# Two-bank score conversions, merged shifts and a spread-out second normalisation in a fused attention and routed-MLP kernel

## The chip, the cores and the metric

The kernel runs on one NeuronCore of a Trainium2 chip. Its time is the device time of one execution in microseconds (us), given as the median over several runs. The profile is of one execution of its own, whose time stands beside the others; "span" is the time from its first to its last instruction. Engine names are those of the profile: PE is TensorE, ACT is ScalarE, DVE is VectorE, POOL is GpSimd, SP is SyncE, which here only issues DMAs.

## The reference

One sequence of 2048 rows of width 448 (bf16) passes through two blocks.

```python
x = A_x
h  = x + A(layernorm(x))         # A: 16 heads of width 28 that share one k and one v
h2 = h + B(layernorm(h))         # B: a routed MLP for 8 rows of the 2048

# A
q = (x @ wq) in 16 heads; k = x @ wk; v = x @ wv          # k, v: 2048 x 28
o = softmax(q k^T / sqrt(28)) v, per head; return concat(o) @ wo
# B
r = x @ w_r; idx = the 8 rows with the largest r
y = (silu(x[idx] @ w_gate) * (x[idx] @ w_up)) @ w_down * sigmoid(r[idx])
return x + scatter_add(zeros, idx, y)                     # x is the normalised h here
```

So every output row is h + layernorm(h), and 8 rows get an MLP result on top.

## The kernel before, in words

**The order of the work.** `_main` only describes operations: engine, code, a duration, the keys it reads and writes, a priority (the planned time of the event that made it). `_Graph.plan` then runs a list scheduler over these durations and so fixes one static order for each engine; `finish` and `emit` place the semaphore waits. An instruction whose wait lasts longer than planned holds everything that stands behind it on its engine. DMAs are issued by SP in such an order too, and the two gathers and the last scatter by POOL.

**The blocks.** The attention is cut into 16 blocks `b`: a quarter of the queries (`b // 4`, 512 of them) by a group of 4 heads (`b % 4`). A block has 16 tiles `j` of 128 keys; planned time counts 16 units to a block. For each tile PE makes the scores of 4 heads in two halves `p` (two matmuls each, into a pair of PSUM banks), one engine turns scores into bf16 probabilities, and PE multiplies them by V, accumulating in the bank `acc_bank(b)`. A row of ones in V gives the sum of the probabilities, `l`. There are two ways to make the probabilities:

- ACT tiles (`act_unit`, line 845): two exponentials of 128x1024 each, one for each half, over banks 0 and 1 or 2 and 3 in turn; four matmuls with V.
- DVE tiles (`dve_unit`, `shift`, lines 858 and 864): K carries a scale that makes the clamped, converted int16 the bit pattern of a bf16 near the exponential. Each half lies in banks 4 and 5 and takes two conversions of 128x512. Three shifts then add 32, 64 and 96 to the 128x2048 integers of level 0 and write levels 1 to 3, and all four levels are multiplied by four differently scaled copies of V, 16 matmuls in all. The buffer `Y` has three places.

`groups[b]` says how many of a block's 16 tiles are DVE tiles: 4, but 3 in blocks 5, 9 and 13.

**After a block** (`post_block`): DVE copies the accumulator to `Ot` (line 636), a DMA writes its four rows `l` to DRAM, another reads them back as 128x16 (`Lc`), DVE folds them into a running minimum and maximum `Lmn`, `Lmx` (lines 640, 642; they decide at the end whether an exact version of everything has to run) and takes reciprocals, two more DMAs spread these over the partitions (`Rb`), and POOL multiplies (line 648, `On`).

**After four blocks** (`out_proj`, four row tiles `t` of 128 rows): PE multiplies by wo, DVE adds x (`hbuf`), takes mean and variance, POOL raises to the power -0.5 (line 670), DVE makes the output row `outf`, a normalised row `xn` in bf16 (line 680), and the router value `r` of each row. The four tiles of blocks 0 to 3, of 4 to 7 and of 8 to 11 stand about 2 units apart in blocks 5, 9 and 13. After the fourth, one DMA writes `outf` to the output and one writes `xn` to a DRAM scratch.

**The router.** After 12 row tiles (`first_row`, `first_max`), PE brings 1536 router values to 12 partitions, three DMAs lay them out as one row of 1536, and DVE's MAX8 and FIND_INDEX8 (lines 713, 715) find the best 8. In block 15 (`second_top`) the 8 indices go to 8 partitions (`idc`, line 727) and POOL gathers (line 735) these rows from the output (`extc`) and from the scratch (`xnc`). The last 512 rows are handled in the tail: normalised there, searched together with the best 8, then the MLP for 8 rows and a scatter by POOL.

`last_w` (lines 741, 749) computes w_r times wo and w_r times x for the tail.

Of the kernel before, what the change touches and what calls it, by code (L numbers as in the profile page):

```python
# [7 lines left out]
ALU = mybir.AluOpType  # L8
# [222 lines left out]
def _main(nc, G, sb, ps, psb, flag, scr, xs, A_x, A_wq, A_wk, A_wv, A_wo, B_w_r, B_w_gate, B_w_up, B_w_down, out,  # L231
# [79 lines left out]
    r12 = sb("r12", [12, 128], F32)  # L311
    r_row = xnF[0:1, 0:3072].bitcast(F32)
# [11 lines left out]
    iota_n = sb("iota_n", [128, 5], F32)  # L324
    iota_i = sb("iota_i", [128, 2, NT], I32)
# [95 lines left out]
    for i in range(4):  # L421
# [26 lines left out]
    G.op(DV, lambda e: e.memset(Lmn[:, :], 1.0), 90, writes=["Lmn"])  # L448
    G.op(DV, lambda e: e.memset(Lmx[:, :], 1.0), 90, writes=["Lmx"])
# [158 lines left out]
    def post_block(b):  # L608
        g, qb, rb = b % 4, b // 4, b % 2
        u = 16 * (b + 1) + 2.6  # L610
# [24 lines left out]
        else:  # L635
# [4 lines left out]
        G.op(DV, lambda e: e.tensor_tensor(Lmn[:, :], Lmn[:, :], Lc[:, rb, :], ALU.min), 85,  # L640
             reads=["Lmn", ("Lc", rb)], writes=["Lmn"])
        G.op(DV, lambda e: e.tensor_tensor(Lmx[:, :], Lmx[:, :], Lc[:, rb, :], ALU.max), 85,
             reads=["Lmx", ("Lc", rb)], writes=["Lmx"])
        if not last:
            G.op(DV, lambda e: e.reciprocal(Lc[:, rb, :], Lc[:, rb, :]), 200, reads=[("Lc", rb)], writes=[("Lc", rb)])
            dma(scr[b, 1].rearrange("i (r k) -> (i r) k", k=16), Lc[:, rb, :], [("scr1", b)], reads=[("Lc", rb)])
# [8 lines left out]

    def out_proj(qb, k):
        t = qb * 4 + k
        hr = t % 4
        bank = misc_bank(4 * qb + 5)
# [4 lines left out]
        G.op(DV, lambda e: e.tensor_tensor(hbuf[:, hr, :], ps[:, bank, 0:D], x_sb[:, t, 0:D], ALU.add), dvt(D),  # L664
             reads=[pk(bank), ("x", t)], writes=[("h", hr)])
        G.op(DV, lambda e: e.bn_stats(bn6[:, t, :], hbuf[:, hr, :]), dvt(D), reads=[("h", hr)], writes=[("bn6", t)])  # L666
# [3 lines left out]
        G.op(PO, lambda e: e.tensor_tensor(st[:, t, 4:5], st[:, t, 7:8], nhalf[:, 0:1], ALU.pow), 570,  # L670
             reads=[("st7", t), "nhalf"], writes=[("st4", t)])
        G.op(DV, lambda e: e.tensor_scalar(st[:, t, 5:6], st[:, t, 4:5], 1.0, None, ALU.add), 80,
             reads=[("st4", t)], writes=[("st5", t)])
        G.op(DV, lambda e: e.scalar_tensor_tensor(st[:, t, 6:7], mv[:, t, 0:1], -1.0, st[:, t, 4:5],
                                                  ALU.mult, ALU.mult), 85,
             reads=[("mv", t), ("st4", t)], writes=[("st6", t)])
        G.op(DV, lambda e: e.tensor_scalar(outf[:, t, :], hbuf[:, hr, :], st[:, t, 5:6], st[:, t, 6:7],
                                           ALU.mult, ALU.add), 420,
             reads=[("h", hr), ("st5", t), ("st6", t)], writes=[("outf", t)])
        G.op(DV, lambda e: e.tensor_scalar(xn[:, t, :], hbuf[:, hr, :], st[:, t, 4:5], st[:, t, 6:7],  # L680
                                           ALU.mult, ALU.add), 420,
             reads=[("h", hr), ("st4", t), ("st6", t)], writes=[("xn", t)])
        G.op(DV, lambda e: e.scalar_tensor_tensor(junk[:, :], hbuf[:, hr, :], st[:, t, 4:5], w_rb[:, :],  # L683
                                                  ALU.mult, ALU.mult, accum_out=st[:, t, 2:3]), 700,
             reads=[("h", hr), ("st4", t), "w_rb"], writes=["junk", ("st2", t)])
        G.op(DV, lambda e: e.scalar_tensor_tensor(x_sb[:, t, D + 2:D + 3], st[:, t, 6:7], sw[:, 0:1], st[:, t, 2:3],
                                                  ALU.mult, ALU.add), 85,
             reads=[("st6", t), "sw", ("st2", t)], writes=[("r", t)])
        if k == 3:
            evs.append(dma(out_v[:, t - 3:t + 1, :], outf[:, t - 3:t + 1, :], [("out", qb)],  # L690
                           reads=[("outf", i) for i in range(t - 3, t + 1)]))
            dma(xs[(t - 3) * 128:(t + 1) * 128, :].rearrange("(n p) d -> p n d", p=128), xn[:, t - 3:t + 1, :],
                [("xs", qb)], reads=[("xn", i) for i in range(t - 3, t + 1)])
# [10 lines left out]
    def first_row(bank):  # L704
        G.op(PE, mm(ps[0:12, bank, 0:128], x_sb[:, 0:12, D + 2], ident[:, :], True, True), 200,
             reads=[("r", t) for t in range(12)] + ["ident"], writes=[pk(bank)])
        G.op(DV, lambda e: e.tensor_copy(r12[:, :], ps[0:12, bank, 0:128]), 200, reads=[pk(bank)], writes=["r12"])
        for c in range(3):
            dma(r_row[0:1, 512 * c:512 * c + 512].rearrange("o (t p) -> o t p", p=128), r12[4 * c:4 * c + 4, :],
                [("r_row", c)] + (old if c == 0 else []), reads=["r12"] + (old if c else []))  # L710

    def first_max():
        G.op(DV, lambda e: e.max(top8[:, 0, :], r_row[:, :]), 1700, reads=[("r_row", c) for c in range(3)],
             writes=[("top8", 0)])
        G.op(DV, lambda e: e.max_index(idx8[:, 0, :], top8[:, 0, :], r_row[:, :]), 1760,
             reads=[("r_row", c) for c in range(3)] + [("top8", 0)], writes=[("idx8", 0)])
# [3 lines left out]
    def second_top():  # L720
# [6 lines left out]
        G.op(DV, lambda e: e.tensor_scalar(idc[:, :], ps[0:8, bank, 0:1], 0.0, 1535.0, ALU.max, ALU.min), 70, reads=[pk(bank)], writes=["idc"])  # L727
# [6 lines left out]
        for src, dst, nm, rd in ((out[0, 0:1536, :], extc, "extc", "out"), (xs, xnc, "xnc", "xs")):  # L734
            G.op(PO, lambda e, src=src, dst=dst: e.indirect_dma_start(
                dst[:, 0:D], None, src, bass.IndirectOffsetOnAxis(ap=idc[:, 0:1], axis=0)), 1000, dma=True,
                reads=["idc"] + old + [(rd, q) for q in range(3)], writes=[nm])

    def last_w():
        for g in range(4):  # L740
            G.op(DV, lambda e, g=g: e.scalar_tensor_tensor(junk[:, :], wo_pad[:, g, 0:D], 1.0, w_rb[:, :],
                                                           ALU.mult, ALU.mult, accum_out=wor[:, g:g + 1]), 600,
                 reads=["wo_pad", "w_rb"] + wok, writes=["junk", ("wor", g)])
# [4 lines left out]
        for k in range(4):  # L748
            G.op(DV, lambda e, k=k: e.scalar_tensor_tensor(junk[:, :], x_sb[:, 12 + k, 0:D], 1.0, w_rb[:, :],
                                                           ALU.mult, ALU.mult, accum_out=xw[:, k:k + 1]), 600,  # L750
                 reads=[("x", 12 + k), "w_rb"], writes=["junk", ("xw", k)])
# [61 lines left out]
    for b in range(5, NB, 4):  # L813
        groups[b] = 3
# [38 lines left out]
    def dve_unit(m, b, j, p, t):  # L853
# [3 lines left out]
        for k in range(2):  # L857
            G.op(DV, lambda e, k=k: e.tensor_scalar(Y[:, n, 0, p + 2 * k, :].bitcast(I16), ps[:, 4 + k, :], 0.0,  # L858
                                                    32639.0 - 3 * STEP, ALU.max, ALU.min), 610, reads=[pk(4 + k)],
                 writes=[("Y", n, 0, p + 2 * k)], prio=t - 2)  # L860

    def shift(m, v):
        n = m % NY
        G.op(DV, lambda e: e.tensor_scalar(Y[:, n, v, :, :].bitcast(I16), Y[:, n, 0, :, :].bitcast(I16),  # L864
                                           v * STEP, None, ALU.add), 610,
             reads=[("Y", n, 0, k) for k in range(4)], writes=[("Y", n, v, k) for k in range(4)])

    def dve_pv(m, v, b, j, f, l):
# [3 lines left out]
             reads=[("Y", n, v, k) for k in range(4)] + [("V", j // 4), "V1"], writes=[pk(acc_bank(b))], form=2)  # L872
# [18 lines left out]
    for b in range(NB):  # L891
# [10 lines left out]
    at(16 * 14 + 5.0, first_top)  # L902
    at(16 * 14 + 9.0, first_max)
# [42 lines left out]
    else:  # L946
        events.sort(key=lambda t: t[0])
        for t, fn in events:
# [175 lines left out]
```

## Time and profile before

| | us |
|---|---|
| median of 3 runs | 412.21 (412.16 to 412.69) |
| the profiled execution: its own time | 414.31 |
| its span, first to last instruction | 412.2 |
| busy in the span: PE, DVE, ACT, POOL | 352.7, 366.0, 381.1, 51.3 |
| granted TensorE clock, mean over the span | 0.973 |

Busy time is the share of the span in which at least one instruction of the engine runs. Consecutive instructions on ACT and DVE overlap by some tens of nanoseconds, so the mean duration of one, times the count, is more than the busy time. In a group's line, "x396 | 368.1, 1089" means 396 instructions, 368.1 us busy in all, 1089 ns the mean of one. The first ACT exponential starts at 12.4 us and the last one ends at 386.2; what lies after that is called the tail.

### The profile page before, as it was taken

To read this page: it belongs to the slowest core of one execution; us is meant where nothing else is said; L and a number is where in the kernel's file an instruction comes from. 1 tells how busy PE (TensorE), PEld (TensorE's weight loads), DVE (VectorE), ACT (ScalarE), POOL (GpSimd) and SP (SyncE) were. 2 spreads that over 40 slices of the span, in tenths; PEclk is the share of its full clock that TensorE was granted. 3 is DMA by queue.
4 is the path that set the end of the run, shared out by engine and by line. 5 is a ranking of instruction groups with operands and counts; after the bars stand their busy time and mean duration, and the time that the engine had idled before them with its cause. 6 is when DMAs were issued, how large, how long until landed. Compare 5 with 4: busy or idle time off the path is not lost.

```text
span 412.2 us, 8124 instructions
## 1 busy us (share of the span) xinstructions
PE 352.7 (86%) x3335; PEld 110.9 (27%) x3335; DVE 366.0 (89%) x785; ACT 381.1 (92%) x429; POOL 51.3 (12%) x76
## 2 busy tenths in 40 slices
PE   8899989898897998888798997988888987898845
PEld 7333222222221221222122222222222221222235
DVE  5998899999899998989999999889989998998281
ACT  4899998999999999999999999999999999999640
POOL 7231000101010020101000120101010130213000
PEclk9999999999999998999999999999999999999955
DMA  7696000100000002000000002000000002001000
GB/s 197 161 228 160 1 2 4 53 4 28 1 28 0 26 6 91 28 3 26 2 27 2 22 8 92 28 2 29 4 27 2 29 0 94 27 4 29 2 34 18
DMA packets 17845, 15.74 MB, mean 38 GB/s; under 512 B 6440, under 2 KB 14924, under 8 KB 17804
## 3 DMA queue, kind: packets, MB, share of 16 engines
q1 hardware_dynamic: 17708, 15.16, 13.4%
q8 instruction: 27, 0.44, 0.5%
q14 instruction: 14, 0.11, 0.1%
q0 software_dynamic: 96, 0.02, 0.0%
HBM read 11.70 MB, written 3.47 MB: 37 GB/s over the span
## 4 chain that ended last, share of the span: by engine, by line
ACT 54%; PE 27%; DVE 16%; issue 1%; DMA 1%; POOL 0%; SPq 0%; POOLq 0%; DVEq 0%
ACT P L845 53%; PE ps L351 27%; DVE Y L858 7%; DVE Y L864 6%; DVE Ot L636 1%; DMA Lc<-l_scr 1%; DVE bn L772 1%; ACT K L527 0%; DVE idx L972 0%; ACT xn L789 0%; POOL out_dram L1038 0%; DVE On L630 0%; SPq L365 0%; DVE wq_sb L1037 0%; DVE ra L778 0%
## 5 line engine op out<-in xcount | busy, mean ns | idle before, releaser
L845 ACT ACTIVATE P<-ps 128x1024 bf16<-128x1024 f32 x396 | 368.1, 1089 | 6.3 <-PE ps L351 4.3
L351 PE MATMUL ps<-Q,K 64*128 64x512 bf16 x1024 | 183.0, 386 | 42.1 <-ACT P L845 29.5
L858 DVE TENSOR_SCALAR Y<-ps 128x512 int16<-128x512 f32 x232 | 149.5, 680 | 13.2 <-PE ps L351 12.7
L864 DVE TENSOR_SCALAR Y<-Y 128x2048 int16<-128x2048 int16 x174 | 119.0, 715 | 1.5
L351 PEld LDWEIGHTS ps<-Q,K 64*128 64x128 bf16 x1024 | 43.9, 93 | 188.2 <-ACT P L845 146.8
L351 PE MATMUL ps<-P,Vs 128*32 128x512 bf16 x792 | 78.4, 390 | 0.0
L351 PE MATMUL ps<-Y,Vs 128*32 128x512 bf16 x928 | 77.7, 382 | 0.1
L648 POOL TENSOR_TENSOR On<-Ot,Rb 128x512 bf16<-128x512 f32 x15 | 22.4, 1496 | 235.9 <-DMA Rb<-l_scr 235.9
L351 PEld LDWEIGHTS ps<-P,Vs 128*32 128x32 bf16 x792 | 20.1, 93 | 46.1 <-issue 45.5
L351 PEld LDWEIGHTS ps<-Y,Vs 128*32 128x32 bf16 x928 | 23.6, 95 | 24.5 <-issue 12.4
L351 PE MATMUL ps<-xnT,wq_pad 112*128 112x512 bf16 (+1 forms) x68 | 19.3, 377 | 1.4 <-DVE Ot L636 1.2
L351 PE MATMUL ps<-wo_pad,On 128*128 128x448 bf16 (+1 forms) x64 | 17.8, 358 | 2.6 <-DVE Ot L636 1.8
L670 POOL TENSOR_TENSOR st<-st,nhalf 128x1 f32<-128x1 f32 x12 | 9.3, 773 | 65.2 <-DVE st L668 65.2
L466 DVE TENSOR_SCALAR Q<-ps,qone 128x512 bf16<-128x512 f32 x15 | 10.8, 722 | 2.4 <-PE ps L351 2.4
L636 DVE COPY Ot<-ps 128x512 f32<-128x512 f32 x15 | 10.3, 686 | 1.0 <-PE ps L351 0.6
L351 PE MATMUL ps<-ident 128*128 128x128 bf16 x72 | 7.6, 287 | 1.8 <-POOL ident L380 1.8
L683 DVE SCALAR_TENSOR_TENSOR junk<-hbuf,st,w_rb 128x448 bf16<-128x448 f32 x12 | 8.1, 677 | 0.0
L664 DVE TENSOR_TENSOR hbuf<-ps,x_sb 128x448 f32<-128x448 f32 x12 | 7.4, 616 | 0.6 <-PE ps L351 0.6
L666 DVE BATCH_NORM_STATS2 bn<-hbuf 128x6 f32<-128x448 f32 x12 | 7.4, 620 | 0.1
L351 PEld LDWEIGHTS ps<-ident 128*128 128x128 bf16 x72 | 6.9, 134 | 1.8 <-POOL ident L380 1.8
L351 PEld LDWEIGHTS ps<-wo_pad,On 128*128 128x128 bf16 x64 | 4.2, 97 | 11.8 <-issue 7.9
L351 PEld LDWEIGHTS ps<-xnT,wq_pad 112*128 112x128 bf16 x68 | 4.4, 98 | 10.2 <-issue 4.2
(175 smaller groups left out, 171.9 us busy)
## 6 DMA issues: line engine op xcount, KB each, us to landing
Rb<-l_scr SPq DMA_DIRECT2D x15, 256.0 KB
wg_sb<-in_B_w_gate_dram SPq DMA_DIRECT2D x1, 1568.0 KB, 12.7
wu_sb<-in_B_w_up_dram SPq DMA_DIRECT2D x1, 1568.0 KB, 19.6
wd_sb<-in_B_w_down_dram SPq DMA_DIRECT2D x1, 1568.0 KB, 23.3
x_sb<-in_A_x_dram SPq DMA_DIRECT2D x3, 448.0 KB, 6.2
out_dram<-x_sb SPq DMA_DIRECT2D x3, 448.0 KB, 3.1
xn_scr<-xn SPq DMA_DIRECT2D x3, 448.0 KB, 4.0
x_sb<-in_A_x_dram SPq DMA_DIRECT2D x4, 112.0 KB, 2.1
```

The lines of the kernel that those rows point to most:

```text
L351: return lambda e: e.matmul(o, lhsT=l, rhs=r, start=start, stop=stop)
L466: G.op(DV, lambda e: e.tensor_scalar(Q[:, b % 4, :], ps[:, bank, :], qone[:, 0:1], None, ALU.add), dvt(512), reads=[pk(bank), "qone"], wri ...
L636: G.op(DV, lambda e: e.tensor_copy(Ot[:, rb, :], ps[:, acc_bank(b), :]), dvt(512), reads=[pk(acc_bank(b))], writes=[("Ot", rb)], prio=u - 30)
L648: G.op(PO, lambda e: e.tensor_tensor(On[:, qb % 2, g, :], Ot[:, rb, :], Rb[:, rb, :], ALU.mult), 1270, reads=[("Ot", rb), ("Rb", rb)], wri ...
L664: G.op(DV, lambda e: e.tensor_tensor(hbuf[:, hr, :], ps[:, bank, 0:D], x_sb[:, t, 0:D], ALU.add), dvt(D), reads=[pk(bank), ("x", t)], writ ...
L666: G.op(DV, lambda e: e.bn_stats(bn6[:, t, :], hbuf[:, hr, :]), dvt(D), reads=[("h", hr)], writes=[("bn6", t)])
L670: G.op(PO, lambda e: e.tensor_tensor(st[:, t, 4:5], st[:, t, 7:8], nhalf[:, 0:1], ALU.pow), 570, reads=[("st7", t), "nhalf"], writes=[("st ...
L683: G.op(DV, lambda e: e.scalar_tensor_tensor(junk[:, :], hbuf[:, hr, :], st[:, t, 4:5], w_rb[:, :], ALU.mult, ALU.mult, accum_out=st[:, t, ...
L772: G.op(DV, lambda e: e.bn_stats(bn6[:, t, :], ps[:, bank, 0:D]), dvt(D), reads=[pk(bank)], writes=[("bn6", t)])
L845: G.op(AC, lambda e: e.activation(P[:, sl, :, :], ps[:, b0:b0 + 2, :], ACT.Exp, bias=EBIAS, scale=OCT), 905, reads=[pk(b0), pk(b0 + 1)], w ...
L858: G.op(DV, lambda e, k=k: e.tensor_scalar(Y[:, n, 0, p + 2 * k, :].bitcast(I16), ps[:, 4 + k, :], 0.0, 32639.0 - 3 * STEP, ALU.max, ALU.mi ...
L864: G.op(DV, lambda e: e.tensor_scalar(Y[:, n, v, :, :].bitcast(I16), Y[:, n, 0, :, :].bitcast(I16), v * STEP, None, ALU.add), 610, reads=[( ...
```

## The change

- Scores: a DVE half is converted by one instruction over both banks (128x2x512) in place of two.
- Shifts: two in place of three. The first makes level 1 from level 0 (128x2048); the second adds 64 to levels 0 and 1 together and writes levels 2 and 3 (128x4096). It reads what the first wrote.
- `groups[b]` is 4 in all blocks: three more DVE tiles, three fewer ACT tiles.
- `out_proj` is spread (`ln_block`): one row tile in each of blocks 5 to 12, two in each of blocks 13 and 14, in the bank that is free there. `xn` and its bulk write are gone: the scratch gets the f32 row of `hbuf` with the two numbers of its normalisation in two more columns, one DMA of 128x450 for each row tile, and only the 8 gathered rows are normalised, by a new DVE instruction in block 15. The output is written in pairs of row tiles.
- The router's first search works in two levels: MAX8 and FIND_INDEX8 over 12 partitions of 128, a DMA that makes a row of 96 values, two that bring the 96 positions to 8 partitions, the search over 96, and a selection of the position by comparison.
- The minimum and maximum of `l` become running sums of `l` and 1/l, on POOL (on DVE for the last block); their test at the end is two instructions in place of four.
- `last_w` also waits for block 3's `l` to be written.
- The scratch tensors for `l`, for the rows and for the positions are parts of one DRAM tensor.

```diff
-        for k in range(2):
-            G.op(DV, lambda e, k=k: e.tensor_scalar(Y[:, n, 0, p + 2 * k, :].bitcast(I16), ps[:, 4 + k, :], 0.0,
-                                                    32639.0 - 3 * STEP, ALU.max, ALU.min), 610, reads=[pk(4 + k)],
-                 writes=[("Y", n, 0, p + 2 * k)], prio=t - 2)
+        G.op(DV, lambda e: e.tensor_scalar(Y[:, n, 0, p:p + 3:2, :].bitcast(I16), ps[:, 4:6, :], 0.0,
+                                           32639.0 - 3 * STEP, ALU.max, ALU.min), 1140, reads=[pk(4), pk(5)],
+             writes=[("Y", n, 0, p)], prio=t - 2)
...
-        G.op(DV, lambda e: e.tensor_scalar(Y[:, n, v, :, :].bitcast(I16), Y[:, n, 0, :, :].bitcast(I16),
-                                           v * STEP, None, ALU.add), 610,
+        G.op(DV, lambda e: e.tensor_scalar(Y[:, n, v:2 * v, :, :].bitcast(I16), Y[:, n, 0:v, :, :].bitcast(I16),
+                                           v * STEP, None, ALU.add), 70 + 535 * v,
...
-        for v in (1, 2, 3):
+        for v in (1, 2):
             at(t + 1.6 + 0.5 * v, shift, m, v)
...
-    for b in range(5, NB, 4):
-        groups[b] = 3
...
-        G.op(DV, lambda e: e.tensor_tensor(Lmn[:, :], Lmn[:, :], Lc[:, rb, :], ALU.min), 85, ...)
-        G.op(DV, lambda e: e.tensor_tensor(Lmx[:, :], Lmx[:, :], Lc[:, rb, :], ALU.max), 85, ...)
+        G.op(DV, lambda e: e.reciprocal(Li[:, rb, :], Lc[:, rb, :]), 170, ...)
+        G.op(LE, lambda e: e.tensor_tensor(Lsi[:, :], Lsi[:, :], Li[:, rb, :], ALU.add), 150, ...)
+        G.op(LE, lambda e: e.tensor_tensor(Ls[:, :], Ls[:, :], Lc[:, rb, :], ALU.add), 150, ...)
...
+    def ln_block(qb, k):
+        return 4 * qb + 5 + (k if qb < 2 else k // 2)
...
-        G.op(DV, lambda e: e.tensor_scalar(xn[:, t, :], hbuf[:, hr, :], st[:, t, 4:5], st[:, t, 6:7],
-                                           ALU.mult, ALU.add), 420, ...)
...
-        if k == 3:
-            evs.append(dma(out_v[:, t - 3:t + 1, :], outf[:, t - 3:t + 1, :], [("out", qb)], ...))
-            dma(xs[(t - 3) * 128:(t + 1) * 128, :].rearrange("(n p) d -> p n d", p=128), xn[:, t - 3:t + 1, :], ...)
+        dma(xs[t * 128:(t + 1) * 128, :], hbuf[:, hr, :], [("xs", t)], reads=[("h", hr), ("h4", hr), ("h6", hr)],
+            lat=3000.0)
+        if k % 2:
+            evs.append(dma(out_v[:, t - 1:t + 1, :], outf[:, t - 1:t + 1, :], [("out", qb, k)], ...))
...
-        G.op(DV, lambda e: e.max(top8[:, 0, :], r_row[:, :]), 1700, ...)
+        G.op(DV, lambda e: e.max(top8[:, 0, :], v_row[:, :]), 180, reads=["v_row"], writes=[("top8", 0)])
...
+        G.op(DV, lambda e: e.scalar_tensor_tensor(ohq[:, :], iota96[:, :], sel3[:, 0:1], prow[:, :], ALU.is_equal,
+                                                  ALU.mult, accum_out=posc[:, :]), 220, ...)
...
+        G.op(DV, lambda e: e.tensor_scalar(xnc[:, 0:D], hc[:, 0:D], hc[:, D:D + 1], hc[:, D + 1:D + 2], ALU.mult,
+                                           ALU.add), 420, reads=["hc"] + old, writes=["xnc"])
...
-                 reads=["wo_pad", "w_rb"] + wok, writes=["junk", ("wor", g)])
+                 reads=["wo_pad", "w_rb", ("scr0", 3)] + wok, writes=["junk", ("wor", g)])
...
-                    at(16 * b + 37.5 + k * 2.0, out_proj, b // 4, k)
+                    at(16 * ln_block(b // 4, k) + (9.5 if b < 11 else 4.5 + 6.0 * (k % 2)), out_proj, b // 4, k)
...
-    at(16 * 14 + 5.0, first_top)
-    at(16 * 14 + 9.0, first_max)
+    at(16 * 14 + 14.0, first_top)
+    at(16 * 15 + 1.0, first_max)
     at(16 * 15 + 5.0, second_top)
```

More of the change, by code (lines that the diff above doesn't have):

```diff
@@ L689, in out_proj @@
-        if k == 3:
[L690 to L693, printed above, removed]
+        G.op(PO, lambda e: e.tensor_tensor(s4, st[:, t, 7:8], nhalf[:, 0:1], ALU.pow), 570,
+             reads=[("st7", t), "nhalf"], writes=[("h4", hr)])
@@ L750, in last_w @@
                                                            ALU.mult, ALU.mult, accum_out=xw[:, k:k + 1]), 600,
[L751 removed]
+                 reads=[("x", 12 + k), "w_rb", ("scr0", 3)], writes=["junk", ("xw", k)])
     LB = (4, 5, 6, 0)
@@ L871, in dve_pv @@
                   for i in range(4)], 216,
-             reads=[("Y", n, v, k) for k in range(4)] + [("V", j // 4), "V1"], writes=[pk(acc_bank(b))], form=2)
+             reads=([("Y", n, v)] if v else [("Y", n, 0, 0), ("Y", n, 0, 1)]) + [("V", j // 4), "V1"],
+             writes=[pk(acc_bank(b))], form=2)
     for n, (b, j, t) in enumerate(act_tiles):
```

136 lines of the change are left out of this document (79 added, 57 removed).

## The prediction

> **What bounds the kernel now.** I read the page's busy shares and chain first, then the groups, then windows cut at the accumulator copies of line 636.
>
> ```profile
> span 412.2 us, 8124 instructions
> ...
> PEclk9999999999999998999999999999999999999955
> ...
> ACT 54%; PE 27%; DVE 16%; issue 1%; DMA 1%; POOL 0%; SPq 0%; POOLq 0%; DVEq 0%
> ...
> L845 ACT ACTIVATE P<-ps 128x1024 bf16<-128x1024 f32 x396 | 368.1, 1089 | 6.3 <-PE ps L351 4.3
> L858 DVE TENSOR_SCALAR Y<-ps 128x512 int16<-128x512 f32 x232 | 149.5, 680 | 13.2 <-PE ps L351 12.7
> L864 DVE TENSOR_SCALAR Y<-Y 128x2048 int16<-128x2048 int16 x174 | 119.0, 715 | 1.5
> ...
> L351 PE MATMUL ps<-Y,Vs 128*32 128x512 bf16 x928 | 77.7, 382 | 0.1
> ```
>
> The chain names three engines, so the group's idle column decides: before its 396 exponentials ACT sat idle for 6.3 us in all, while they kept it busy for 368.1. One therefore costs 368.1/396 = 0.930 us of ACT time (the mean of 1089 ns counts the overlap of neighbours twice). The windows say the same by stage: first the whole stretch of exponentials and the tail, then block 12 (four DVE tiles) and block 13 (three, and four row tiles of `out_proj`), last the sum over blocks 2 to 15 (67.9 to 386.2 us, in 14 windows).
>
> ```profile
> 12.40:386.20 373.80, 328.74 (x2987) 91.73 (x2986) 345.55 (x695) 368.07 (x396) 41.56 (x37) 1.00 0.13 34
> 386.20:412.20 26.00, 13.82 (x244) 9.94 (x242) 12.70 (x60) 7.86 (x23) 0.93 (x1) 0.63 0.07 21
> ...
> 295.10:317.60 22.50, 19.60 (x184) 5.27 (x182) 20.25 (x33) 22.41 (x26) 1.77 (x1) 1.00 0.05 15
> 317.60:342.30 24.70, 22.15 (x184) 5.88 (x182) 24.02 (x68) 24.33 (x27) 4.59 (x5) 1.00 0.05 14
> ...
> sum 318.30, PE 279.39 PEld 74.89 DVE 293.72 ACT 312.98 POOL 34.58; mean PE 19.96 PEld 5.35 DVE 20.98 ACT 22.36 POOL 2.47
> ```
>
> After the length come busy PE, weight loads, DVE, ACT, POOL. ACT is full in both kinds of block (22.41 of 22.50, 24.33 of 24.70); DVE is nearly full only where `out_proj` stands (24.02 of 24.70), and PE is a tenth below. Time is 12.4 before the first exponential, 373.8 with them, 26.0 of tail, and 2.1 outside the span (414.31 - 412.2). Fewer exponentials are the only large gain on offer; all ACT idleness in blocks 2 to 15 is 318.3 - 313.0 = 5.3 us.
>
> **The change part by part.**
>
> *Three ACT tiles become DVE tiles.* Six exponentials go: 6 x 0.930 = **-5.6 us**, provided DVE and PE keep pace. PE trades three products with P for twelve with Y, net 9 groups of four matmuls; from the Y row (77.7/232 = 0.335 us per group) that is +3.0 us of PE in blocks 5, 9 and 13, against some 2.5 us of PE idleness in each of them, and the bunched output projections leave these blocks.
>
> *DVE's budget.* The cost of an instruction in a queue is the step to the next one, not its duration:
>
> ```profile
> 125.03 1.90 DVE L864 TENSOR_SCALAR Y<-Y 128x2048 int16<-128x2048 int16 x3
> ...
> 129.93 0.69 DVE L864 TENSOR_SCALAR Y<-Y 128x2048 int16<-128x2048 int16 x1
> ...
> L617 DVE TENSOR_SCALAR Ot<-ps x2: 415/420/425, 387.2 to 387.6; 128x256 f32<-128x256 f32 x2
> ...
> L466 DVE TENSOR_SCALAR Q<-ps,qone 128x512 bf16<-128x512 f32 x15 | 10.8, 722 | 2.4 <-PE ps L351 2.4
> L636 DVE COPY Ot<-ps 128x512 f32<-128x512 f32 x15 | 10.3, 686 | 1.0 <-PE ps L351 0.6
> ...
> L680 DVE TENSOR_SCALAR xn<-hbuf,st 128x448 bf16<-128x448 f32 x12 | 6.1, 506 | 0.0
> ...
> L645 DVE RECIPROCAL Lc<-Lc 128x16 f32<-128x16 f32 x15 | 3.7, 244 | 0.0
> L642 DVE TENSOR_TENSOR Lmx<-Lmx,Lc 128x16 f32<-128x16 f32 x16 | 2.7, 167 | 0.0
> L640 DVE TENSOR_TENSOR Lmn<-Lmn,Lc 128x16 f32<-128x16 f32 x16 | 2.7, 166 | 2.6 <-DMA Lc<-l_scr 2.5
> ...
> L749 DVE SCALAR_TENSOR_TENSOR junk<-x_sb,w_rb 128x448 bf16<-128x448 bf16 x4 | 2.5, 621 | 0.1
> ...
> L741 DVE SCALAR_TENSOR_TENSOR junk<-wo_pad,w_rb 128x448 bf16<-128x448 bf16 x4 | 2.4, 605 | 0.0
> ...
> L715 DVE FIND_INDEX8 idx<-top,xnT 1x8 uint32<-1x1536 f32 x1 | 1.7, 1739 | 0.0
> L713 DVE MAX8 top<-xnT 1x8 f32<-1x1536 f32 x1 | 1.7, 1732 | 0.0
> ...
> 67.90:386.20 318.30, 33.26 (x72) 0.99 0.08 23
> ```
>
> Three shifts in a row take 1.90, one 0.69: a step of 0.605. From 256 to 512 columns a PSUM read goes from 420 to 686 ns, so 512 columns are 0.532 and the fixed part of a step is 0.073. No row has a two-bank conversion or a 128x4096 shift; the bounds are 2 x 0.605 = 1.21 (nothing saved) and 2 x 0.532 + 0.073 = 1.137. I take 1.137, since the fixed part is read from like instructions. A DVE tile falls from 7 x 0.605 = 4.24 us to 2 x 1.137 + 0.605 + 1.137 = 4.02 (or 4.24 again). In all: 58 tiles save 12.8, three more cost 12.1, the rows `xn` give 6.1, minimum and maximum 5.0, the long searches 3.4 less about 1 for five short instructions, and `last_w` (eight instructions, 2.5 + 2.4) comes in from the first 40 us: 293.7 - 9.2 = about 284.5 us of DVE for blocks 2 to 15, in which ACT then wants 307.
>
> By block: four tiles 16.1, `Q` 0.65, `Ot` 0.61, reciprocal 0.17 make 17.5. A row tile costs (33.26 - 6.1)/12 = 2.3 for what touches `hbuf` (the last row) and about 0.4 for its small instructions: 2.7. ACT needs 24 x 0.930 = 22.3 in every block. So blocks 5 to 12 hold 20.2, well inside; block 4 with `last_w` 17.5 + 4.9 = 22.4, over by 0.1; blocks 13 and 14 with two row tiles 22.9, over by 0.6 each, and block 14 has the first search as well. I book **+0.4** for block 4 and **+1.0** for 13 and 14 (0 if block 15's slack takes it, 3 if PE is held at each eviction).
>
> *Stalls that go.* Where four row tiles stand together, DVE runs late afterwards:
>
> ```profile
> 349.32 0.18 DVE L640 TENSOR_TENSOR Lmn<-Lmn,Lc 128x16 f32<-128x16 f32 x1 [1.80 <-DMA Lc<-l_scr]
> ```
>
> Here it waits 1.80 for a small read that was issued behind two writes of 448 KB; the new writes are half as large and spread. The reciprocal now stands at the head of that wait, with conversions, shifts and, behind them, PE's products queued as before. I book **-1.8**, and 5.3 (all idleness) as the bound.
>
> *A new wait in block 15.* The order of the changed program has, after `idc`: shift, two small ones, shift of 4096, one small, two conversions, then the normalisation of the gathered rows, and behind it the last tile's two shifts; PE's last products with Y wait for these, and behind them in PE's order stand the scores for ACT's last four exponentials.
>
> ```profile
> 368.96 0.14 DVE L727 TENSOR_SCALAR idc<-ps 8x1 uint32<-8x1 f32 x1
> ...
> 371.09 1.63 POOL L735 DMA_INDIRECT xnT<-xn_scr,idc  x1 [0.30 <-issue]
> ...
> xnT<-out_dram,idc POOLq DMA_INDIRECT x1, 2.7
> xnT<-xn_scr,idc POOLq DMA_INDIRECT x1, 5.8
> ```
>
> The second gather landed at 371.09 + 5.8 = 376.9, that is 7.8 after `idc` (369.1); with the first one's 2.7 it would be 4.7. DVE comes to the new instruction 0.6 + 0.1 + 1.14 + 0.1 + 2.27 = 4.2 after `idc`. The wait is 0.5 to 3.6; I take 1.0, as the competing `Rb` transfer now starts before the gathers, and book **+0.6** after some slack on PE.
>
> *Sums on POOL.* Thirty additions of 128x16, beside shifts:
>
> ```profile
> L670 POOL TENSOR_TENSOR st<-st,nhalf x12: 537/548/1161, 139.5 to 338.6; 128x1 f32<-128x1 f32 x12
> ...
> L864 DVE TENSOR_SCALAR Y<-Y x174: 628/685/1769, 42.8 to 379.6; 128x2048 int16<-128x2048 int16 x174
> ```
>
> The longest shift took 1769 ns against a median of 685, so something holds shifts. [...] From rows alone: about 0.36 shifts start per us (122 in 340), so an addition of at most 0.54 meets 0.2 of them and delays each by 0.27 on average; 30 x 0.05 = 1.6 at most, less than the 5.0 that DVE sheds. On the path: **0**.
>
> *The rest.* The prologue is the same; the tail loses two small instructions and gains a reciprocal: 0. The 96-value search waits for DMAs that are covered by four conversions and shifts in the new order: 0; if not, 2.
>
> Sum: -5.6 + 0.4 + 1.0 - 1.8 + 0.6 = -5.4. The profiled execution would go from 414.3 to 408.9 (span 406.8); its span is within 0.1 of the median of the runs, so I predict 412.2 - 5.4 = **406.8 us**.
>
> **The rivals.**
>
> *DVE becomes loose and ACT never waits.* All 5.3 us of idleness go too: 412.2 - 5.6 - 5.3 = 401.3. For it: the load of every block from 5 to 12 falls under ACT's. Against: part of the idleness lies at block 2, before any of this.
>
> *The gather holds DVE.* The wait is 3.6 and all of it arrives at ACT: 406.8 - 0.6 + 3.6 = 409.8. For it: the row of 5.8. Against: `Rb` no longer runs beside the gathers to the same extent. [...]
>
> *PE sets the pace* (slower). Over blocks 2 to 15 PE idles 318.3 - 279.4 = 38.9 us. If these gaps are inherent (waits for its own order, changes between kinds of matmul), the 3.0 us of added products are simply added: 412.2 + 3.0 = 415.2. It decides as soon as PE's idleness stays above 318.3 - 282.4 = 35.9. Against it:
>
> ```profile
> PE ps L351 <- ACT P L845: 29.5, 91, 0.5
> ...
> DVE Y L858 <- PE ps L351: 12.7, 22, 1.8
> ```
>
> 29.5 us of PE's waiting are for ACT, in 91 short pieces, and shrink with ACT's work; for it, DVE already waits 12.7 for PE.
>
> *The merging saves nothing.* Tiles stay at 4.24: DVE holds 293.7 + 12.7 - 9.5 = 297 of ACT's 307 and, with blocks 13 and 14 at 23.8, loses some 1.5 in each of them, 0.8 in block 4, and about 0.2 in each of the eight others: 406.8 + 5 = 411.8.
>
> **How the numbers follow.** Forecast, 404.5 to 409.0: 0.56. ACT never waits, 401.3 to 404.5: 0.15. Gather, 409.0 to 411.4: 0.13. Merging saves nothing, 411.0 to 413.0: 0.06. PE sets the pace, above 413: 0.10. The range 403.0 to 411.2 leaves out half of the second case and the last two, about 0.2. About 0.2% (0.8 us) is what a measurement can tell from no change: faster than 411.4 are the first three and little else, 0.84; within it 0.05; slower 0.11.
>
> **What would show it.** Right: 390 exponentials with the same 0.93 us each and no more than 6 us idle before them; conversions of about 1.22 us (1.137 and the overlap of 0.08), shifts of 0.69 and 1.22 in equal number; 22.3 to 22.8 us from one accumulator copy to the next in all blocks from 5 on. Wrong: more than 10 us of ACT idleness; DVE idle over 2 us before the 8x448 normalisation; blocks 13 and 14 longer than 24 us; or PE over 21.5 us busy in each block with ACT waiting for it.

## The result and the profile after

The changed kernel takes 406.61 us (median of 6 runs, 404.94 to 406.84) against 412.19 (median of 6, 411.81 to 414.61): a ratio of 0.985, 95% interval 0.982 to 0.988. A second series gave 406.26 against 413.39, 0.983 (0.980 to 0.986). Over all series the shortest of 51 runs of the kernel before took 411.14 us, the longest of 12 runs of the changed kernel 407.29. The forecast was 406.8.

The page of the kernel after: span, granted clock, chain, then the costliest groups (busy us, mean ns | idle before it and who ended that).

```profile
span 404.9 us, 8047 instructions
...
PEclk9999999999999999999999999999999999999955
...
ACT 61%; PE 18%; DVE 17%; POOL 1%; issue 1%; POOLq 0%
...
L868 ACT ACTIVATE P<-ps 128x1024 bf16<-128x1024 f32 x390 | 361.9, 1085 | 5.3 <-PE ps L360 4.1
...
L880 DVE TENSOR_SCALAR Y<-ps 128x1024 int16<-128x1024 f32 x122 | 148.1, 1214 | 15.1 <-PE ps L360 14.9
```

390 exponentials in place of 396, each at the same 361.9/390 = 0.928 us; 5.3 us of idleness before them in place of 6.3. PE's part of the chain fell from 27 to 18%, ACT's rose: more of the kernel runs at ACT's pace.

The windows of the kernel after: the stretch of the exponentials and the tail; block 9, which is like blocks 6 to 12; then blocks 13 and 14; last the sum over blocks 2 to 15. Columns are length, then busy PE, weight loads, DVE, ACT, POOL, then the granted clock.

```profile
11.80:378.50 366.70, 327.61 (x3017) 92.37 (x3015) 337.07 (x498) 361.89 (x390) 51.84 (x67) 1.00 0.13 39
378.50:404.90 26.40, 14.38 (x249) 10.32 (x248) 12.72 (x60) 7.84 (x22) 0.93 (x1) 0.62 0.07 22
...
221.40:243.60 22.20, 20.06 (x186) 5.51 (x186) 20.68 (x31) 22.19 (x25) 2.83 (x4) 1.00 0.08 25
...
310.10:333.50 23.40, 20.98 (x188) 5.61 (x188) 21.96 (x38) 22.94 (x25) 4.00 (x5) 1.00 0.13 43
333.50:359.00 25.50, 21.94 (x201) 6.11 (x201) 25.06 (x47) 24.61 (x28) 3.72 (x5) 1.00 0.12 40
...
sum 311.90, PE 279.11 PEld 75.72 DVE 290.11 ACT 307.29 POOL 45.10; mean PE 19.94 PEld 5.41 DVE 20.72 ACT 21.95 POOL 3.22
```

The stretch shrank from 373.8 to 366.7 us. In block 9 ACT is busy for 22.19 of 22.20 us, with DVE at 20.68 and PE at 20.06: that block can't be shorter with its 24 exponentials. Blocks 13 and 14, with two row tiles each, lose 0.5 and 0.9 us of ACT time. The tail is 0.4 longer.

From profile to profile the own time falls by 7.6 us (414.31 to 406.75), between medians by 5.6. Of the 7.6, 0.6 lie ahead of the first exponential (12.4 against 11.8 us); the profiles below start it anywhere between 11.3 and 12.4, so this is scatter. Another part is in the profile before, of which this is one more window:

```profile
157.70:161.10 3.40, 3.40 (x18) 0.52 (x18) 3.40 (x6) 2.67 (x3) 0.00 (x0) 0.50 0.59 196
```

For 3.4 us the granted clock is 0.50, and ACT is busy for 2.67 of them. The profile after has no such window in the loop. That execution was one of the longer runs, so the terms below are compared with care for about 2 us.

### The profile page after: what moved, and what is told of

It reads as the page before. It is cut to its first block, busy times and chain, and to the rows that moved or that the text cites. A ratio compares the mean times of both kernels' runs of the same rounds, so it can differ in the third digit from the quotient of the medians.

```text
span 404.9 us, 8047 instructions
## 1 busy us (share of the span) xinstructions
PE 351.5 (87%) x3371; PEld 111.3 (27%) x3371; DVE 357.6 (88%) x586; ACT 374.9 (93%) x423; POOL 62.2 (15%) x112
## 4 chain that ended last, share of the span: by engine, by line
ACT 61%; PE 18%; DVE 17%; POOL 1%; issue 1%; POOLq 0%
ACT P L868 61%; PE ps L360 18%; DVE Y L880 7%; DVE Y L886 5%; POOL hbuf L689 1%; DVE Ot L650 1%; DVE bn L797 1%; DVE junk L697 0%; DVE hbuf L683 0%; DVE x_sb L695 0%; DVE Q L479 0%; DVE wo_pad L771 0%; DVE bn L685 0%; ACT K L540 0%; DVE idx L995 0%
## 5 line engine op out<-in xcount | busy, mean ns | idle before, releaser
L868 ACT ACTIVATE P<-ps 128x1024 bf16<-128x1024 f32 x390 | 361.9, 1085 | 5.3 <-PE ps L360 4.1
L360 PE MATMUL ps<-Q,K 64*128 64x512 bf16 x1024 | 180.8, 384 | 35.7 <-ACT P L868 27.5
L880 DVE TENSOR_SCALAR Y<-ps 128x1024 int16<-128x1024 f32 x122 | 148.1, 1214 | 15.1 <-PE ps L360 14.9
L360 PE MATMUL ps<-Y,Vs 128*32 128x512 bf16 x976 | 84.8, 383 | 3.1 <-DVE Y L886 3.1
L360 PE MATMUL ps<-P,Vs 128*32 128x512 bf16 x780 | 77.2, 388 | 0.0
L659 POOL TENSOR_TENSOR Ls<-Ls,Lc 128x16 f32<-128x16 f32 x15 | 8.9, 596 | 189.3 <-DMA Lc<-h_scr 189.3
L663 POOL TENSOR_TENSOR On<-Ot,Rb 128x512 bf16<-128x512 f32 x15 | 19.7, 1315 | 76.3 <-DMA Rb<-h_scr 76.3
L689 POOL TENSOR_TENSOR hbuf<-st,nhalf 128x1 f32<-128x1 f32 x12 | 9.5, 790 | 20.2 <-DVE st L687 20.2
L697 DVE SCALAR_TENSOR_TENSOR junk<-hbuf,w_rb 128x448 bf16<-128x448 f32 x12 | 8.1, 676 | 0.0
L580 DVE BATCH_NORM_STATS2 bn<-x_sb 128x6 f32<-128x448 bf16 x12 | 7.0, 604 | 0.0
```

What stands on the lines that cost most here:

```text
L360: return lambda e: e.matmul(o, lhsT=l, rhs=r, start=start, stop=stop)
L659: G.op(LE, lambda e: e.tensor_tensor(Ls[:, :], Ls[:, :], Lc[:, rb, :], ALU.add), 150, reads=["Ls", ("Lc", rb)], writes=["Ls"])
L689: G.op(PO, lambda e: e.tensor_tensor(s4, st[:, t, 7:8], nhalf[:, 0:1], ALU.pow), 570, reads=[("st7", t), "nhalf"], writes=[("h4", hr)])
L697: G.op(DV, lambda e: e.scalar_tensor_tensor(junk[:, :], h, s4, w_rb[:, :], ALU.mult, ALU.mult, accum_out=st[:, t, 2:3]), 700, reads=[("h", ...
L868: G.op(AC, lambda e: e.activation(P[:, sl, :, :], ps[:, b0:b0 + 2, :], ACT.Exp, bias=EBIAS, scale=OCT), 905, reads=[pk(b0), pk(b0 + 1)], w ...
L880: G.op(DV, lambda e: e.tensor_scalar(Y[:, n, 0, p:p + 3:2, :].bitcast(I16), ps[:, 4:6, :], 0.0, 32639.0 - 3 * STEP, ALU.max, ALU.min), 114 ...
```

## The experiments

Twelve kernels ran, four to a series. Each time is a median of 5 to 12 runs; its ratio is to the kernel before in the same series, whose medians were 412.54, 412.96 and 413.39 us. The changed kernel itself ran only in the first measurement and in the third series; runs 1 to 8 are set against it by their ratios. Every edit also lets the list scheduler fix a new order, so a run can differ from its base in more places than the lines shown.

**1. The move of tiles undone.**

```diff
+    for b in range(5, NB, 4):
+        groups[b] = 3
```

> The changed kernel with 3 DVE tiles again in blocks 5, 9 and 13: 396 exponentials instead of 390, all else changed. Theory (the number of exponentials sets the time, the rest only makes room): six more at 0.93 us, less up to 1 us of waits because DVE has 12 us less to do: 411.0 to 412.2 us. Rival (lighter DVE work is the gain): DVE falls by 12 us, so 406.6 or less. Rival (the spread of the output projections is the gain): no change, 406.0 to 407.0.

413.78 us, ratio 1.002 (1.001 to 1.004). So all the rest of the change, without the three tiles, gains nothing: it is slower than the kernel before by 0.2%. The direction is the theory's, but its range of 411.0 to 412.2 was missed: the size (about 7 us against the changed kernel) is more than the 5.6 of six exponentials. Both rivals, which had 407 or less, fell.

```profile
11.60:384.50 372.90, 325.66 (x2985) 92.72 (x2984) 332.45 (x486) 367.71 (x396) 48.16 (x67) 1.00 0.13 38
384.50:412.30 27.80, 13.89 (x244) 9.94 (x241) 12.70 (x60) 7.84 (x23) 0.93 (x1) 0.62 0.07 22
```

Of these two windows, stretch and tail, the first is 6.2 longer than the changed kernel's: 367.71 - 361.89 = 5.8 of exponentials and 0.4 of waits. The tail is 1.4 longer, but not by its work: the last scatter starts 22.8 us after the last exponential here (407.3) and 23.0 in the changed kernel (401.5), and lands 2.9 and 3.0 later. What is longer is the rest up to the end of the span, 5.0 us against 3.4; the other profiles have 2.8 to 3.6. So that is this one execution and not the edit. That leaves about 6 of the 7 us with a place in these windows.

**2. The move of tiles alone, in the kernel before.**

```diff
-    for b in range(5, NB, 4):
-        groups[b] = 3
```

> The kernel before with 4 DVE tiles in all blocks and nothing else changed: 390 exponentials, DVE load up by 3 x 4.24 = 12.7 us to about 306 of the 307 us that ACT then wants, and the bunched row tiles stay in blocks 5, 9 and 13. Theory: the 5.6 us are eaten for the larger part by waits in and after these three blocks, 409 to 413 us. Rival (exponentials alone, DVE has room anyway): 406.6 us. Rival (DVE sets the time): 412.2 + 12.7 less its present idleness in the loop, 415 us or more.

417.41 us, ratio 1.013 (1.010 to 1.016), worse than the theory's range and where the rival that DVE sets the time had it (415 or more). The windows are blocks 5 and 9, where the bunched row tiles now stand beside four DVE tiles:

```profile
132.90:160.80 27.90, 24.29 (x204) 6.13 (x202) 27.48 (x73) 25.41 (x28) 3.45 (x5) 1.00 0.10 34
225.10:253.00 27.90, 24.29 (x204) 6.14 (x202) 27.49 (x73) 25.41 (x28) 3.44 (x5) 1.00 0.10 34
```

DVE is busy for 27.5 of 27.9 us and ACT idles 2.5 in each. In the page of this kernel the group of the exponentials reads

```profile
L843 ACT ACTIVATE P<-ps 128x1024 bf16<-128x1024 f32 x390 | 362.9, 1072 | 15.6 <-PE ps L351 14.0
```

15.6 us idle in all against 6.3: it cost 9.3 us of waits to save 5.2 of exponentials. PE is named because ACT waits for its scores, but PE is idle itself for 3.6 us in each of the two blocks, and its waits for DVE's shifts, which are not among those of 0.3 us or more in the kernel before, come to 3.6 us in all.

**3. The old conversions and shifts in the changed kernel.**

```diff
-        G.op(DV, lambda e: e.tensor_scalar(Y[:, n, 0, p:p + 3:2, :].bitcast(I16), ps[:, 4:6, :], 0.0, ...
+        for k in range(2):
+            G.op(DV, lambda e, k=k: e.tensor_scalar(Y[:, n, 0, p + 2 * k, :].bitcast(I16), ps[:, 4 + k, :], 0.0, ...
...
-        for v in (1, 2):
+        for v in (1, 2, 3):
```

> The changed kernel with conversions of one bank and three shifts of 128x2048 again, so 61 tiles at 4.24 instead of 4.02 us of DVE (13.4 us more in all). Theory (DVE has room in most blocks): ACT waits grow only in blocks 4, 13 and 14 and a little elsewhere, 407.5 to 409.5 us. Rival (merging is the gain, DVE sets the time): 406.6 + 10 or more, 416 us and up. Rival (the merging is worth nothing): 406.6 us within 0.8.

407.65 us, ratio 0.990 (0.987 to 0.993): going by the ratios the merging is worth 0.5 to 0.7%, 2 to 3 us, at the low end of the theory's range. The intervals just overlap with the first one of the changed kernel (0.982 to 0.988), and the medians alone differ by 1.0 us, so the size is uncertain.

```profile
L868 ACT ACTIVATE P<-ps 128x1024 bf16<-128x1024 f32 x390 | 360.6, 1087 | 7.9 <-PE ps L360 6.5
```

2.6 us more idleness before the exponentials, and 1.9 of it behind 340 us, in blocks 14 and 15: the waits there are 1.47, 1.49, 0.17 and 0.28 us here, and 0.67 and 0.84 in the changed kernel.

**4. The row tiles bunched again in the changed kernel.**

```diff
     def ln_block(qb, k):
-        return 4 * qb + 5 + (k if qb < 2 else k // 2)
+        return 4 * qb + 5
...
-                    at(16 * ln_block(b // 4, k) + (9.5 if b < 11 else 4.5 + 6.0 * (k % 2)), out_proj, b // 4, k)
+                    at(16 * b + 37.5 + k * 2.0, out_proj, b // 4, k)
```

> The changed kernel with the four row tiles of each output projection close together again in blocks 5, 9 and 13, at the old planned times; writes stay one for each row tile. Theory (spreading removes waits of ACT in and after these blocks): between 2.0 and 3.5 us come back, 408.6 to 410.1 us. Rival (the spread is the whole gain): 412 us. Rival (it is worth nothing since DVE is light enough now): 406.6 us within 0.8.

411.80 us, ratio 0.998 (0.997 to 1.000): 1.3% over the changed kernel, more than the theory's 2.0 to 3.5 us and nearly the whole gain, as the rival had it. So the merging alone doesn't make room for the fourth tile. The loss isn't the same in the three blocks: block 9 loses 0.4 us of ACT time (24.56 busy of 25.00), block 5 loses 3.9 (24.56 of 28.50), and most of a stretch at a granted clock of 0.50 lies in it (155.4 to 162.2 us, in which ACT is busy for 3.19 of 6.80; the mean clock of the block is 0.89), and in block 13 ACT is busy for 24.93 of 27.1 us:

```profile
318.00:345.10 27.10, 24.66 (x210) 6.57 (x208) 25.95 (x59) 24.93 (x27) 3.84 (x7) 1.00 0.19 63
```

**5. Five tiles in blocks 2 and 3.**

```diff
+    groups[2] = groups[3] = 5
```

> The changed kernel with 5 DVE tiles in blocks 2 and 3, which have no row tiles: 386 exponentials. Theory (the number of exponentials sets the time while DVE has room): 4 x 0.93 = 3.7 us less, minus about 1 us in each of the two blocks, where DVE then wants 17.5 + 4.0 = 21.5 us and ACT 22 x 0.93 = 20.5: 403.0 to 404.9 us. Rival (DVE is the limit again): 406.6 us or more.

409.02 us, ratio 0.991 (0.988 to 0.994): four exponentials fewer and slower than the changed kernel. The theory's range was missed; the rival that DVE is the limit again (406.6 or more) holds. Blocks 2, 3 and 4:

```profile
66.60:90.00 23.40, 20.77 (x200) 5.64 (x198) 23.30 (x26) 20.32 (x23) 4.69 (x6) 1.00 0.08 26
90.00:111.20 21.20, 19.50 (x186) 5.04 (x186) 20.79 (x23) 19.88 (x22) 3.03 (x3) 1.00 0.05 14
111.20:137.00 25.80, 21.97 (x190) 5.63 (x188) 25.18 (x40) 23.28 (x26) 2.24 (x3) 0.93 0.04 13
```

DVE is busy for 69.3 of 70.4 us and ACT idles 3.1, 1.3 and 2.5, where the changed kernel has 1.4, 0.1 and 0.5: block 2 has waits without a fifth tile already, and block 4 has `last_w`. My estimate took each block alone; the lateness of one is handed to the next. The third window also has a granted clock of 0.93, and 1.0 of its 2.5 lies in the stretch at 0.50 (ACT is busy for 2.39 of the 3.40 us from 129.1 on).

**6. The running sums on DVE.**

```diff
-        LE = DV if b == NB - 1 else PO
+        LE = DV
```

> The changed kernel with the running sums of l and 1/l on DVE in every block, 30 additions of 128x16 back from POOL. Theory (they cost DVE steps of about 0.085 us, 2.5 us in all, and no block runs over but 4, 13 and 14): 406.6 us within 0.8. [...] Rival (DVE is the limit): 409 us.

405.29 us, ratio 0.982 (0.980 to 0.984), below the theory's 405.8 to 407.4 and far from the rival's 409. That spoke for a gain, and the form of shift below moved the same way, first in the changed kernel, then here:

```profile
L886 DVE TENSOR_SCALAR Y<-Y 128x4096 int16<-128x4096 int16 x61 | 76.6, 1256 | 0.9
```

```profile
L886 DVE TENSOR_SCALAR Y<-Y 128x4096 int16<-128x4096 int16 x61 | 74.6, 1223 | 0.8
```

61 shifts are 2.0 us shorter together. But the ratio lies within the second interval of the changed kernel (0.980 to 0.986), and the ninth run takes the verdict back: with the sums on DVE, and `last_w` early, the time was that of the changed kernel beside it.

**7. `last_w` without its added wait.**

```diff
-                 reads=["wo_pad", "w_rb", ("scr0", 3)] + wok, writes=["junk", ("wor", g)])
+                 reads=["wo_pad", "w_rb"] + wok, writes=["junk", ("wor", g)])
...
-                 reads=[("x", 12 + k), "w_rb", ("scr0", 3)], writes=["junk", ("xw", k)])
+                 reads=[("x", 12 + k), "w_rb"], writes=["junk", ("xw", k)])
```

> The changed kernel without the added wait of last_w, so that its eight DVE instructions (4.9 us) may run in the first two blocks as before. Theory (block 4 lost only some 0.1 us by them, and the first blocks lose as much): 406.6 us within 0.8. Rival (they hold block 4, which is over its limit with them): 405.5 us or less. Rival (they delay keys and first DVE tiles in blocks 0 and 1): 407.6 us or more.

406.10 us, ratio 0.983 (0.981 to 0.985): no difference that these runs resolve.

**8. A tile moved from block 13 to block 2.**

```diff
+    groups[2], groups[13] = 5, 3
```

> The changed kernel with 5 DVE tiles in block 2 and 3 in block 13, 390 exponentials as before it. Theory (ACT's waits of 1.4 and 1.6 us in blocks 13 and 14 come from DVE having two row tiles beside four tiles): at least 1 us of them goes, block 2 gains at most 1 us: 405.0 to 406.2 us. Rival (they come from each row tile's way over POOL and back, whatever DVE's load): 406.6 us within 0.6 or above.

407.29 us, ratio 0.987 (0.984 to 0.990): no gain, as the rival had it. The 1.4 and 1.6 us of the expectation are not ACT's waits: those are 0.5 and 0.9 in the windows of the kernel after, so that less was to be won. Block 2, then blocks 13 and 14:

```profile
66.20:89.30 23.10, 20.80 (x200) 5.62 (x198) 23.00 (x27) 20.36 (x23) 4.76 (x6) 1.00 0.08 27
311.90:335.70 23.80, 21.23 (x180) 5.71 (x180) 22.95 (x41) 23.80 (x27) 4.07 (x5) 1.00 0.13 42
335.70:357.80 22.10, 20.24 (x187) 5.53 (x187) 20.83 (x43) 22.09 (x25) 4.44 (x5) 1.00 0.14 46
```

The mechanism is the theory's: with a tile less, ACT is busy for 23.80 of 23.80 us in block 13 and 22.09 of 22.10 in block 14, with the row tiles' way over POOL still there, which speaks for DVE's load as the cause of their waits. But this profile has another 1.7 us of ACT idleness in a stretch at a granted clock of 0.50 (172.6 to 176.0 us), and in block 2 ACT idles 2.7 us now. In the kernel after it was 20.80 - 19.39 = 1.4:

```profile
66.60:87.40 20.80, 19.32 (x180) 5.16 (x178) 20.10 (x24) 19.39 (x22) 4.87 (x6) 1.00 0.09 30
```

**9. Sums on DVE and `last_w` early together** (the edits of 6 and 7).

> The changed kernel with the running sums on DVE in all blocks and last_w free of its added wait, 390 exponentials. Theory (the sums on POOL held shifts and the row tiles' way over POOL: with them on POOL shifts lost 3.0 us above their usual 1.22 and 0.69, with them on DVE 0.8): 1 to 2 us under the changed kernel of the same call, 404.6 to 405.8 us. Rival (that difference was scatter): equal to the changed kernel within 0.5 us.

**10. The same, with a tile moved from block 13 to block 4.**

```diff
+    groups[4], groups[13] = 5, 3
```

> The same as the run with sums on DVE and last_w early, with 5 DVE tiles in block 4 and 3 in block 13. Theory (block 4 without last_w has 17.7 us of DVE work and takes a tile where block 2, which starts with DVE behind, could not): waits of blocks 13 and 14 go without new ones in block 4, 0.5 to 1.5 us under that run. Rival (any block with 5 tiles loses what block 13 gains): equal within 0.5 us.

**11. The same as 9, with a fifth tile in block 4.**

```diff
+    groups[4] = 5
```

> The same as the run with sums on DVE and last_w early, with 5 DVE tiles in block 4 and 4 in block 13: 388 exponentials. Theory (two exponentials less are 1.9 us where DVE has room): 0.9 to 1.9 us under that run. Rival (DVE in a block of 5 tiles, 21.7 us against ACT's 20.5, gives back all of it): equal within 0.5 us or slower.

**12. The changed kernel again.**

> The changed kernel itself once more, as the measure for the other kernels of this call: 406.6 us within 0.8 by every theory.

The four ran beside each other: 406.25, 406.79, 406.24 and 406.26 us, with ratios of 0.983, 0.983, 0.982 and 0.983 and intervals of 0.003 to 0.004 on either side. So the runs resolve no difference among them; a gain of 1 us would lie inside the intervals. The theories of runs 9 to 11 had gains, and none shows. The rivals that said "equal within 0.5" hold for runs 9 and 11; run 10 is 0.54 over run 9.

What run 10 gained and lost can be read in its trace. ACT's waits in blocks 13 to 15 before the gathers fall from 1.8 us in run 9 (0.16 + 0.34 + 1.26) to 0.3, those between 130 and 231 us, in which run 9 has none, come to 1.7, and behind the gathers there is a new one. From DVE's and ACT's timelines:

```profile
370.90 1.39 DVE L761 TENSOR_SCALAR xnT<-xnT 8x448 bf16<-8x448 f32 x1 [2.51 <-DMA xnT<-h_scr,idc]
```

```profile
374.97 1.02 ACT L869 ACTIVATE P<-ps 128x1024 bf16<-128x1024 f32 x1 [1.75 <-PE ps L360]
```

The second gather took 5.0 us here (2.2 in the kernel after); DVE waited 2.51 for it, PE 1.32 for DVE's next conversion, and ACT 1.75 for PE. That is the prediction's rival "the gather holds DVE", in another order of the work.

In the eleventh, two more exponentials went and nothing came of it. Its blocks 4 to 6:

```profile
109.50:133.30 23.80, 21.81 (x204) 5.69 (x204) 21.68 (x25) 23.50 (x27) 1.27 (x1) 1.00 0.04 13
133.30:155.50 22.20, 19.84 (x184) 5.46 (x182) 22.20 (x34) 21.62 (x24) 1.82 (x2) 1.00 0.07 24
155.50:177.80 22.30, 19.86 (x184) 5.13 (x186) 21.14 (x32) 21.61 (x24) 1.83 (x2) 1.00 0.10 35
```

Block 4 takes the tile; the bill comes in block 5, where DVE is busy for all 22.20 us and ACT idles 0.6, and 0.7 again in block 6, while in run 9 ACT waits 0.58 in block 4 and then not once before 328 us. Over the whole kernel 1.4 us of exponentials are saved (362.0 to 360.6) and 1.1 of waits come back (5.5 to 6.6). With one row tile in each block from 5 to 12 DVE hands a debt on with little to pay it from.

## Why the prediction was right

*The term that carries it: right.* Six exponentials at 0.93 were booked at -5.6; the busy time of the group fell from 368.1 to 361.9, by 6.2. Undoing only this move costs about 7 us (run 1), so no other part explains the gain by itself.

*DVE has room: right, with a total that was 5.6 us too low.* The step as the unit of cost held: the conversion took 1.214 us (1.22 forecast), the shifts 0.70 and 1.22 where nothing held them. Yet the total of DVE for blocks 2 to 15 came to 290.1, not 284.5. Most of the mis-sized part is in what goes away: I counted the 30 minima and maxima and the 12 rows `xn` at their full durations, though I had just shown that a queue pays some 0.08 less for each, which is 3.4 in all. I also let 58 tiles save 0.22 each, where blocks 2 to 15 hold 53 of them (159 shifts, three to a tile): 1.1 more. And one small instruction of `last_w` (line 771) took 1.23 us in place of 0.17: 1.1 more. By this estimate the three make up the 5.6.

*The spread: mis-sized.* The 1.8 us were a wait of DVE in block 14 of the kernel before, and I took them for ACT's. ACT lost only 22.50 - 21.94 = 0.56 in that block:

```profile
342.30:364.80 22.50, 18.14 (x175) 4.73 (x175) 20.11 (x37) 21.94 (x25) 2.45 (x1) 1.00 0.18 54
```

Booked as -1.8 for stalls that go, the spread is what gives the move its room: about 5 us hang on it (run 4), some 2 on the merging (run 3). I priced it against the waits of the kernel before, and not against those that the fourth tile would have made in blocks 5, 9 and 13 without it (run 2: 2.5 us in each).

*Blocks 4, 13 and 14: right in kind.* +0.4 and +1.0 were booked. Block 4's early or late `last_w` does not show in the time (run 7). Blocks 5 to 12 took 21.9 to 22.7 us each, around the lower edge of the 22.3 to 22.8 named as a sign; block 14 with 25.5, 26 exponentials ending in it, overstepped the sign of 24. Blocks 13 and 14 lose 1.4 us of ACT time against 0.9 in the kernel before (24.70 - 24.33 and 22.50 - 21.94): 0.4 more, where 1.0 was booked.

*The gather in block 15: the wait did not come in this profile, and another did.* From DVE's and POOL's timelines and the DMA issues of the kernel after:

```profile
366.62 0.13 DVE L748 TENSOR_SCALAR idc<-posc 8x1 uint32<-8x1 f32 x1
...
370.60 1.22 DVE L880 TENSOR_SCALAR Y<-ps 128x1024 int16<-128x1024 f32 x1 [0.74 <-PE ps L360]
371.75 0.49 DVE L761 TENSOR_SCALAR xnT<-xnT 8x448 bf16<-8x448 f32 x1
```

```profile
369.08 0.86 POOL L758 DMA_INDIRECT xnT<-h_scr,idc  x1 [0.30 <-issue]
```

```profile
xnT<-h_scr,idc POOLq DMA_INDIRECT x1, 2.2
```

The second gather landed 2.2 us after its issue, at 371.3, 4.5 after `idc`; DVE, held by PE for 0.74 before its last conversion, came to the normalisation 5.0 after `idc` and found the rows there. The reason given for taking the low end, that `Rb` would no longer run beside the gathers, was only half of it: `Rb` was issued at 365.6 and was there by 370.7, so it ran during the first gather and most of the second, and was done before the second landed. The wait is real in other orders: DVE waits for the gather in the profiles of runs 1, 3, 4, 6, 8, 9 and 11, for 0.25 to 1.39 us, and in run 10 for 2.51.

Block 15 nevertheless loses 19.50 - 18.64 = 0.86 us of ACT time, against 0.08 in the kernel before:

```profile
364.80:386.20 21.40, 19.69 (x180) 5.43 (x179) 15.29 (x31) 21.32 (x24) 4.50 (x3) 1.00 0.06 15
```

```profile
359.00:378.50 19.50, 17.68 (x160) 5.01 (x160) 14.33 (x27) 18.64 (x21) 5.75 (x5) 1.00 0.06 17
363.64 14.84 ACT L868 ACTIVATE P<-ps 128x1024 bf16<-128x1024 f32 x16 [0.84 <-PE ps L360]
```

The last line, from ACT's timeline, shows one wait of 0.84 for PE that ends 3 us before `idc`, so before any gather. It comes in runs 5, 7 and 12 too (0.84 to 0.85); what PE's order lacked there was not tried. The +0.6 that was booked thus has about the right size through another wait.

*Sums on POOL: 0 booked, 0 found* (runs 6, 9 and 12). Whether the merged shifts pay for them isn't shown either: the 1.6 us of the prediction were my estimate, which no run shows, and with the sums on DVE the mean of the merged shifts is 1223, 1238 and 1265 ns in the profiles of runs 6, 9 and 11, with the sums on POOL 1256 and 1252 in the two of the changed kernel. Single places show longer times side by side; a power on POOL, issued just after a merged shift began:

```profile
327.72 1.23 DVE L886 TENSOR_SCALAR Y<-Y 128x4096 int16<-128x4096 int16 x1
329.38 0.15 DVE L691 TENSOR_SCALAR st<-hbuf 128x1 f32<-128x1 f32 x1 [0.44 <-POOL hbuf L689]
```

```profile
327.82 1.53 POOL L689 TENSOR_TENSOR hbuf<-st,nhalf 128x1 f32<-128x1 f32 x1 [3.61 <-DVE st L687]
```

Its median over the 12 is 0.55 us; here it took 1.53 and ended 1.63 after the shift's start, and DVE then waited 0.44 for it.

*The other rivals.* That DVE becomes loose and ACT never waits fell: 5.3 us of idleness before the exponentials remain. That merging saves nothing fell too: the forms took what was forecast, and going back to the old ones costs about 2 us (run 3), where that rival put 5.

*PE sets the pace: fell.* PE's idleness in the stretch of exponentials was 373.8 - 328.7 = 45.1 us and is 366.7 - 327.6 = 39.1: it shrank with ACT's work, as its waits for ACT had suggested. In blocks 2 to 15, for which the prediction set the mark at 35.9, it is 311.9 - 279.1 = 32.8.

*Two numbers were right by luck.* I took the span of the profile before (412.2) for the time of a usual run because it agreed with the median. Its own time was 2 us above the median, with the window at a granted clock of 0.50 in it. The sum made against it, 408.9, stands against a measured 406.75 for the profiled run; between medians it fits to 0.2 us. And the four terms for waits, +0.4, +1.0, -1.8 and +0.6, add up to +0.2. Leaving out block 6, where that window lay (0.92 us of ACT idleness before, 0.08 after), the idleness in blocks 2 to 15 went from 4.4 to 4.5 us. The sum fits; of its parts the -1.8 was too large, the +1.0 too, and the +0.6 came from elsewhere.

## What to carry to other kernels

Where two engines share a queue of work and both are nearly full, moving work to the other one, making room on it, and spreading its bursts are one change: here the move alone costs 1.3%, the room alone costs 0.2%, and together they gain 1.5%. Price a move block by block, with the lateness that each block hands to the next, and price the part that makes the room against the waits that the move would bring without it. When the next unit moved gains nothing (run 11), the balance is reached at that place; whether one of the others still has room isn't shown by these runs. A wait counts by what it costs the engine that sets the pace: 1.8 us of DVE's waiting in block 14 were 0.56 of ACT's.

## What the hardware showed

In some profiles the granted TensorE clock falls to 0.50 within the loop for 3.4 us (before, runs 1, 2, 5 and 8) or 6.8 (run 4); its mean over the span is 0.967 to 0.974 in these six. In the profiles of the changed kernel and of runs 3, 6, 7 and 9 to 12, with means of 0.974 to 0.979, there is no such stretch in the loop. In the window of before shown above PE is busy for 3.40 of 3.40 us. The 3.4 us just ahead of it in the kernel before read:

```profile
154.30:157.70 3.40, 1.96 (x16) 0.60 (x18) 3.05 (x10) 3.40 (x5) 0.01 (x1) 1.00 0.23 77
```

PE is busy for 1.96 of 3.40 us there. What brings the clock to 0.50 was not tried, and no run shows it.

A merged shift issued while POOL multiplied took longer, too. From DVE's and POOL's timelines of the kernel after:

```profile
323.20 2.10 DVE L886 TENSOR_SCALAR Y<-Y 128x4096 int16<-128x4096 int16 x1
```

```profile
322.94 1.27 POOL L663 TENSOR_TENSOR On<-Ot,Rb 128x512 bf16<-128x512 f32 x1 [4.68 <-DMA Rb<-h_scr]
```

POOL's multiply ends at 324.21; the shift, issued while it ran, ends 1.09 later, about what an undisturbed one lasts (1.22), and so takes 2.10. The forecast had feared the small sums on POOL; the four shifts of this profile that exceed their usual time most (2.18, 2.10 and 1.57 us against 1.22, 1.42 against 0.69) all began while such a multiply ran, which the kernel before has as well.
